# Three edits to the order of small operations in an attention and feed-forward kernel on one core

## The chip, the core and the metric

The kernel runs on one core of a Trainium2 chip. The metric is device time in microseconds (us) of one execution. Before the change it is 855.39 us, the median of three runs (854.91 to 855.95). The core has a matrix engine (PE; its weight loads are shown as PEld), a vector engine (DVE), a scalar engine (ACT), a general engine (POOL) and SyncE (SP), which issues nearly all DMAs. Each engine works through its own instructions in the order of the program and waits for the others by semaphores.

## The reference

Attention with softmaxes over q and over k, in 8 batches of 8 heads, 576 rows and 64 columns; its output, 4608 tokens of 512 columns, goes through a feed-forward layer with a squared ReLU.

```python
q_s = exp(q - max(q, -1)); q_s /= q_s.sum(-1) + 1e-9
k_s = exp(k - max(k, 2));  k_s /= k_s.sum(2) + 1e-9
kv  = einsum('bhsd,bhse->bhde', k_s, v)
x   = einsum('bhsd,bhde->bhse', q_s, kv).transpose(0, 2, 1, 3).reshape(4608, 512)
h   = maximum(x @ w_in, 0)          # w_in is 512 x 2048
out = (h * h) @ w_out               # w_out is 2048 x 512
```

## The kernel before

**Precision.** The feed-forward products keep single precision by splitting: an operand becomes a rounded part "hi" (a cast or copy on ACT) and a remainder "lo" = value minus hi (a subtraction on DVE, in a few places on POOL). A product is three matmuls: hi by hi, hi by lo, lo by hi.

**Tiles 0 to 4 (t = 0 to WT).** Five tiles of 512 tokens go straight through. Each has 16 chunks f of the hidden dimension. A chunk's order in the program (loop at L1631) is: `first`, 12 matmuls into a bank h, then ReLU and square on ACT into r; `sums_step`; `pairs_first`; the 12 matmuls of `second` for chunk f-2, in four output columns c; `split_g`, which makes gh (ACT) and gl (DVE) from r; `pairs_step`; in tile 4 also `ahead`.

**Attention for later batches runs inside tiles 1 to 4.** A round takes five chunks and serves two pairs of heads. In a tile, chunks 4, 9 and 14 are the last of a round, and hold `x_two` (L997), which stands between the columns c = 2 and c = 3 of `second`: PE multiplies q by kv, into a spare bank (the last 64 rows, tile h_x) and two other banks; ACT copies h_x to xt and the others to x. The next chunk's `first` writes into that spare bank (its matmuls are shown as h_x<-xh,w), so it waits for the copy xt. Chunks 3, 8 and 13 hold `blocks_norm` and `blocks_turn` (DVE: small bst operations, two products q<-q,bst, two transposes qT<-q) at their head, then `kv_of`: PE products kv from ek, DVE ks, ACT kv<-kv,ks; `x_two` needs these. Chunks 2, 7 and 12 hold the second `end_k` (DVE k shift, ACT ek).

**Sums of weights.** From tile 5 on pairs of tiles are done jointly by a seven-product (Strassen-Winograd) scheme, which needs sums of weight blocks. They are made in tiles 1 to 3, nine sets, three per tile (`SUMS_AT`, L1558), by `sums_step` (L1537): `full_sums` and `add_sums` on DVE, then at chunk 4, 9 or 14 `split_sums` (two ACT casts sums_h<-sums), one chunk later `rest_sums` (DVE), then `keep_sums` stores them (wo_sums<-sums_h). The buffers of all these have the tag "w" of a pool with two.

**Tile 4, `ahead` (L1579).** At the ends of chunks it makes the scheme's inputs of the first joint pair: blocks b11, b21, b12, b22 of x; t1 = b12-b11, t2 = b22-t1, t3 = t2-b11, t4 = b21-t2; each is split by `split_x_of` (two casts, two subtractions). t4's differences run on POOL.

**Joint pairs (k = 0, 1).** `first_products` (L1944) goes over eight pairs n of hidden chunks. A pair has seven products of six matmuls; p1, p6, p7 and p4 add up in bank A, p2, p5 and p3 in bank B, with an ACT copy u taken of A, and DVE sums c = B + u between them. Weights and sums for pair n+2 are loaded in pair n; a load own_a for the sums that are made on the spot comes with them, and DVE works on own_a in the pair after. `second_products` then does the second layer.

**Late outputs.** Of k = 0 five output blocks (out_N twice, c22[1], c21 twice) stay in memory and are turned during k = 1's `first_products`: `turned` (L1868) is a DVE transpose o<-c and four DMAs out_dram<-o of 128-byte runs. The transpose writes a tile of tag "gh", of which there are two; `pair_p4` takes its c from the same two. Two blocks go in n = 0, one each in n = 1, 2 and 3, right after p1. c22 is held in the ring "r" of two, where `pair_p2` also puts its c.

Of the kernel before, what the change touches and what calls it, by code (L numbers as in the profile page):

```python
# [336 lines left out]
def attention_ffn(  # L337
# [200 lines left out]
    made = {}  # L538
# [998 lines left out]
    def sums_step(t, f):  # L1537

        j, i = divmod(f, NF // 2)
        j += 2 * (t - 1)  # L1540
        if t >= 1 and j < NF // 2 and i == 3:
            begin_sums(j)
        for key, at in SUMS_AT.get(t, ()):
            if f == at[0]:
                full_sums(key)
            if f == at[1]:
                for n in range(3):
                    add_sums(key, n)
            if f == at[2]:
                add_sums(key, 3)  # L1550
                split_sums(key)
            if f == at[3]:
                rest_sums(key)
            if f == at[4]:
                keep_sums(key)

    THRICE = (2, 3, 4, 5, 6), (7, 8, 9, 10, 11), (12, 13, 14, 15, 15)
    SUMS_AT = {t: list(zip(KEYS[3 * t - 3:3 * t], THRICE)) for t in range(1, WT)}  # L1558
# [20 lines left out]
    def ahead(f, x):  # L1579

        k = range(2)
        if f == 4:
            made["b11"] = [x[:, i, :] for i in k]
            made["b21"] = [x[:, 2 + i, :] for i in k]
            made["b12"], made["b22"] = (
                [slabs[X_RAW + j].bitcast(F32)[:, i, :] for i in k] for j in range(2)
            )
            w_of[0] = weights(0)
            load_weights(0, w_of[0], "a11", "s1", "a12", "s2")
        elif f == 5:  # L1590
            for i in k:
                Y.dma_start(out=slabs[X_RAW + i].bitcast(F32), in_=x_raw[WT + 1, i])
        elif f == 6:
            split_x_of("b11")
        elif f == 8:
            one = cvt.tile([P, 2, M], F32, tag="w", name="t1_0")
            take("t1", V, [one[:, i, :] for i in k], made["b12"], made["b11"])
        elif f == 9:
            split_x_of("t1")
            take("t2", V, made["t1"], made["b22"], made["t1"])  # L1600
        elif f == 10:
            split_x_of("b21")
            take("t3", V, made["b11"], made["t2"], made["b11"])
        elif f == 12:
            split_x_of("t2")
        elif f == 14:
            take("t4", G, made["b21"], made["b21"], made["t2"])
            split_x_of("t3")
        elif f == 15:
            load_weights(0, w_of[0], "s3", "a22", "s4")  # L1610
            split_x_of("b22")
# [19 lines left out]
    for t in range(WT):  # L1631
        x_next, acc = x_tile(t + 1) if t < TB else None, begin_acc(t)
        parts = {}
        for f in range(NF):
            todo = turns[t, f] if t else None
            h = first(t, f, x)
            sums_step(t, f)
            if f < LA:
                parts[f] = split_g(t, f, *h)
            if t == 0:  # L1640
                for work in done:
                    convert(work, f + 1)
                plan.due = f + SOON
                step(1, f)
                plan.due = None
            if todo:
                pairs_first(*todo)
            if f >= LA:
                for c in range(C):
                    second_all(t, f - LA, parts[f - LA], acc, c)  # L1650
                    if c == 2 and todo and todo[1] > 2:
                        b, p = PAIRS_OF[todo[0]][1]
                        if todo[1] == 3:
                            kv_of(b, p - 1, p)
                        else:
                            x_two(b, p, x_next if b == TB else None)
                parts[f] = split_g(t, f, *h)
            if t == 0:
                plan.due = f + SOON
                step_after(1, f, x_next)  # L1660
                plan.due = None
            elif todo:
                pairs_step(*todo)
            if t >= TB and f == (5 if t == TB else 3):
                x_next = load_x(t + 1)
            if t == WT - 1:
                ahead(f, x_next)
        if t == 0:
            plan.run(SEEDS, fill)
        if t < WT - 1:  # L1670
            x = split_x(x_next, t + 1)
            end_tile(t, parts, acc, NF - 2, NF - 1)
            if t == 0:
                load_q(TB, 1)
                load_v(TB, 1)
                begin_k(TB, 0)
# [217 lines left out]
            out.append(u)  # L1894
        return out

    def added(bank_of, u, name):

        c = temp("r", name, bufs=None)
        V.tensor_tensor(out=c, in0=bank_of, in1=u, op=ALU.add)  # L1900
        return c

# [41 lines left out]
    def first_products(k):  # L1944

        old = None
        for n in range(PAIRS):
            if n == 0 and k == 0:
                split_x_of("t4")
                unit(3)  # L1950
            elif n == 0:
                begin_ring()
            z = pair_begin(n)
            pair_p1(z)
            if turned_late:
                turned_late.pop(0)()
            if n == PAIRS - 1:
                load_raw("b11", 1, raw_place("b11"))
            own_sums(n, z.w, 6)
            pair_p2(z)  # L1960
            if n == 0 and turned_late:
                turned_late.pop(0)()
            if n == PAIRS - 1 and k == 0:
                full_sums(late_key)
            if n == 0 and k == 0:
                unit(2)
                begin_ring()
            elif n == 0:
                split_x_of("t4")
                split_x_of("b22")  # L1970
            if old:
                pair_p4(old)
                load_weights(n + 1, w_of.get(n + 1), "a22")
                own_sums(n + 1, w_of.get(n + 1), 1)
                pair_p3(old)
                load_weights(n + 1, w_of.get(n + 1), "s4")
            own_sums(n + 1, w_of.get(n + 1), 2)
            if n == PAIRS - 1:
                load_raw("b11", 2, raw_place("b21"))
                split_step(0)  # L1980
            pair_p6(z)
            if old:
                pair_c12(old)
            own_sums(n + 1, w_of.get(n + 1), 3)
            if n == 0:
                unit(3)
            pair_p5(z)
            own_sums(n + 1, w_of.get(n + 1), 4)
            if n:
                own_sums(n + 2, None, 0)  # L1990
            if n + 2 < PAIRS:
                w_of[n + 2] = weights(n + 2)
                load_weights(n + 2, w_of[n + 2], "a11", "a12", "s2", "s1")
            elif n == PAIRS - 1:
                if k == 0:
                    for i in range(4):
                        add_sums(late_key, i)
                load_raw("b21", 0, raw_place("t2"))
                load_raw("b21", 1, raw_place("t2", 1))
                raw_x = att.tile([P, 4, M], F32, tag="x_next", name=f"raw_b12_{k}")  # L2000
                for j in range(2):
                    load_raw("b12", j, raw_x[:, 2 * j:2 * j + 2, :])
                split_step(1)
            pair_p7(z)
            load_weights(n + 2, w_of.get(n + 2), "s3")
            if n == PAIRS - 3:
                load_raw("b11", 0, *(temp("v", f"raw_b11_{k}_{i}", att, 2) for i in range(2)))
            if 0 < n < 5:
                load_s("s1", 2 * n - 2)
                if n < 4:  # L2010
                    load_s("s1", 2 * n - 1)
            elif n == PAIRS - 1:
                for j in range(2):
                    load_raw("b22", j, raw_place("t3", j))
            old = z
        return old

    def second_products(k, old):
# [26 lines left out]
        for s in range(1, 6 * J):  # L2045
# [21 lines left out]
            if s == 3 * J:  # L2067
                c11 = [added(out_B[m], u1[m], f"c11_{k}_{m}") for m in range(2)]
            elif s == 5 * J - 1:
                for m in range(2):  # L2070
                    turned(c11[m], two, m, "gh", None, (Y,))
            elif s == 5 * J:
                c22 = [added(out_N[m], u3[m], f"c22_{k}_{m}") for m in range(2)]
            elif s == 5 * J + 1:
                for m in range(2):
                    V.tensor_tensor(out=out_N[m], in0=out_N[m], in1=u2[m], op=ALU.add)
            elif s == 5 * J + 2:
                split_step(6 * J + 3)
                turned(c22[0], one, 2, "gh", None, (Y,))
# [84 lines left out]
```

## Time and profile before

| | |
|---|---|
| median of three runs | 855.39 us |
| the profiled execution: its own time, its span | 853.2 us, 851.4 us |
| PE, weight loads, DVE, ACT, POOL busy | 828.0, 664.0, 604.6, 494.3, 142.2 us |
| mean granted PE clock | 0.998 |
| DMA | 158.08 MB, 186 GB/s over the span |

The span runs from the first instruction to the last. A profile is one execution, slower or faster than the median by what single executions differ.

### The profile page before, as it was taken

The numbers are of one execution on the slowest core, as the hardware profiler recorded it, in microseconds if no ns is written. First come the engines' busy times: TensorE is split into PE (matmuls) and PEld (weight loads), VectorE is DVE, ScalarE is ACT, GpSimd is POOL, SyncE is SP. The second block draws the span as 40 slices with busy tenths as digits, with TensorE's granted clock in tenths as the row PEclk, the third lists the DMA queues.
The fourth block names the chain that finished last, engine by engine and source line by source line (L and its number), as shares of the span: only waits on it lengthen the run. The fifth ranks groups of instructions, "written<-read, shape, count | busy, mean of one in ns | idle before, by whom it ended". The sixth has DMA issues, their size and how long they took to land.

```text
span 851.4 us, 12950 instructions
## 1 busy us (share of the span) xinstructions
PE 828.0 (97%) x4411; PEld 664.0 (78%) x4411; DVE 604.6 (71%) x1098; ACT 494.3 (58%) x890; POOL 142.2 (17%) x153
## 2 busy tenths in 40 slices
PE   8999999899999999999999999999999999899997
PEld 7677777688887787787787787888888877688886
DVE  6888965676675685675665585477698977676984
ACT  5988844545555547555555466466754546575442
POOL 4888980001000000000000001000210000000000
PEclk9999999999999999999999999999999999999999
DMA  9993124426536537355536542899866689989455
GB/s 291 378 343 90 31 42 117 105 77 170 148 107 165 134 126 220 82 173 134 154 136 145 192 126 70 271 291 307 298 255 196 199 248 272 287 294 358 127 175 95
DMA packets 230146, 158.08 MB, mean 186 GB/s; under 512 B 147392, under 2 KB 200128, under 8 KB 230080
## 3 DMA queue, kind: packets, MB, share of 16 engines
q1 hardware_dynamic: 224160, 155.55, 60.3%
q10 hardware_dynamic: 5920, 1.71, 0.9%
q8 instruction: 35, 0.57, 0.3%
q14 instruction: 31, 0.25, 0.1%
HBM read 106.95 MB, written 49.81 MB: 184 GB/s over the span
## 4 chain that ended last, share of the span: by engine, by line
PE 59%; DVE 15%; DMA 10%; ACT 6%; SPq 5%; issue 4%; POOL 0%; DVEq 0%; ACTq 0%; POOLq 0%
PE acc L100 14%; PE out L1839 14%; PE h L1302 13%; PE h L100 11%; SPq L100 5%; PE h_x L100 4%; DVE bst L100 4%; DVE q L100 3%; DMA k<-in_k_dram 3%; DVE w L100 2%; DMA own_a<-w_sums 1%; ACT r L100 1%; PE x L100 1%; PE kv L100 1%; DVE qT L100 1%
## 5 line engine op out<-in xcount | busy, mean ns | idle before, releaser
L100 PE MATMUL acc<-w,gh 128*128 128x512 f32 x632 | 198.5, 395 | 0.0
L100 PE MATMUL h<-xh,w 128*128 128x512 f32 x544 | 179.6, 393 | 0.8 <-ACT xh L100 0.8
L1839 PE MATMUL out<-w,w 128*128 128x512 f32 x636 | 148.9, 389 | 0.0
L100 PEld LDWEIGHTS acc<-w,gh 128*128 128x128 f32 x632 | 116.1, 188 | 29.6 <-issue 5.9
L1839 PEld LDWEIGHTS out<-w,w 128*128 128x128 f32 x636 | 119.3, 188 | 25.1 <-DVE w L100 0.2
L100 DVE TENSOR_TENSOR gl<-r,gh 128x512 fp32r<-128x512 f32 x64 | 44.2, 690 | 112.0 <-ACT gh L100 112.0
L100 PE MATMUL acc<-w,gl 128*128 128x512 f32 x316 | 123.1, 389 | 0.0
L100 PEld LDWEIGHTS h<-xh,w 128*128 128x128 f32 x544 | 102.1, 188 | 23.5 <-ACT xh L100 1.3
L100 PE MATMUL h<-xl,w 128*128 128x512 f32 x272 | 106.3, 391 | 0.1
L100 POOL PARTITION_ALL_REDUCE kmx<-km x24 | 22.7, 946 | 361.8 <-DVE km L100 361.8
L1302 PE MATMUL h<-w,w 128*128 128x512 f32 x288 | 69.6, 390 | 1.0 <-DMA w<-w_sums 1.0
L100 PEld LDWEIGHTS acc<-w,gl 128*128 128x128 f32 x316 | 59.3, 188 | 12.5
L1302 PEld LDWEIGHTS h<-w,w 128*128 128x128 f32 x288 | 53.9, 188 | 13.0 <-DMA w<-w_sums 1.5
L100 PEld LDWEIGHTS h<-xl,w 128*128 128x128 f32 x272 | 51.1, 188 | 11.9 <-DVE xl L100 1.5
L100 ACT ACTIVATE c<-c 128x512 f32<-128x512 f32 x76 | 48.1, 633 | 19.8 <-DVE c L100 18.2
L100 ACT ACTIVATE kv<-kv,ks 64x64 f32<-64x64 f32 x64 | 19.8, 309 | 58.7 <-DVE ks L100 56.7
L100 ACT CAST gh<-r 128x512 fp32r<-128x512 f32 x64 | 39.7, 621 | 17.0 <-PE acc L100 15.4
L1302 PE MATMUL h<-w,ring 128*128 128x512 f32 x192 | 46.7, 391 | 2.8 <-DMA ring<-w_sums 1.7
L100 ACT ACTIVATE q<-q 128x576 f32<-128x576 f32 (+1 forms) x32 | 21.5, 672 | 46.7 <-DVE q L100 39.3
L100 ACT CAST w<-w 128x1024 fp32r<-128x1024 f32 (+1 forms) x38 | 37.9, 1003 | 15.2 <-PE out L1839 8.7
L100 DVE TENSOR_TENSOR c<-h,u 128x512 f32<-128x512 f32 x48 | 33.0, 687 | 18.1 <-ACT u L100 17.0
L100 ACT ACTIVATE r<-h 128x512 f32<-128x512 f32 x68 | 40.1, 590 | 9.2 <-PE h L100 8.6
(229 smaller groups left out, 1387.9 us busy)
## 6 DMA issues: line engine op xcount, KB each, us to landing
w<-wo_sums SPq DMA_DIRECT2D x64, 256.0 KB, 3.4
g_b<-c SPq DMA_DIRECT2D x60, 256.0 KB, 4.2
w<-g_b SPq DMA_DIRECT2D x18, 512.0 KB, 7.1
raw<-in_moe_w_in_dram SPq DMA_DIRECT2D x16, 512.0 KB, 8.1
raw<-in_moe_w_out_dram SPq DMA_DIRECT2D x16, 512.0 KB, 8.6
w<-w_sums SPq DMA_DIRECT2D x32, 256.0 KB, 5.0
w_sums<-w SPq DMA_DIRECT2D x30, 256.0 KB, 3.2
v<-in_v_dram SPq DMA_DIRECT2D x56, 128.0 KB, 3.1
```

The lines of the kernel that those rows point to most:

```text
L100: getattr(self.eng, op)(*map(real, args), **{k: real(a) for k, a in kwargs.items()})
L1302: nc.tensor.matmul(out=out.real(), lhsT=a[:, k * P:(k + 1) * P].real(), rhs=m[k].real(), start=(begin and k == 0 and i == 0), stop=(k == 1 ...
L1839: nc.tensor.matmul(out=banks[name][m].real(), lhsT=a[:, m * P:(m + 1) * P].real(), rhs=b[:, i, :].real(), start=fresh and j == i == k == 0 ...
```

## The change

Three edits. (1) `split_sums` is taken out of `sums_step` and called from a new `sums_after` at the end of the same chunk, behind `second`, `x_two`, `split_g` and `pairs_step`. (2) In `ahead`, b11's split and t1's differences move to the end of chunk 7 (from 6 and 8), t3's differences to chunk 12 ahead of t2's split (from 10), and t4's differences go from POOL to DVE, behind t3's split. (3) The late outputs skip pair n = 1: c22[1] goes in n = 2 and c21 in n = 3 and 4; c22[1] is held in the tile "qt".

```diff
             if f == at[2]:
                 add_sums(key, 3)
-                split_sums(key)
...
+    def sums_after(t, f):
+
+        for key, at in SUMS_AT.get(t, ()):
+            if f == at[2]:
+                split_sums(key)
...
-        elif f == 6:
+        elif f == 7:
             split_x_of("b11")
-        elif f == 8:
             one = cvt.tile([P, 2, M], F32, tag="w", name="t1_0")
             take("t1", V, [one[:, i, :] for i in k], made["b12"], made["b11"])
...
         elif f == 10:
             split_x_of("b21")
+        elif f == 12:
             take("t3", V, made["b11"], made["t2"], made["b11"])
-        elif f == 12:
             split_x_of("t2")
         elif f == 14:
-            take("t4", G, made["b21"], made["b21"], made["t2"])
             split_x_of("t3")
+            take("t4", V, made["b21"], made["b21"], made["t2"])
...
                 pairs_step(*todo)
+            sums_after(t, f)
...
-    def added(bank_of, u, name):
+    def added(bank_of, u, name, place=("r", ffn, None)):
 
-        c = temp("r", name, bufs=None)
+        tag, pool_of, bufs = place
+        c = temp(tag, name, pool_of, bufs)
...
-            if turned_late:
+            if n != 1 and turned_late:
                 turned_late.pop(0)()
...
-                c22 = [added(out_N[m], u3[m], f"c22_{k}_{m}") for m in range(2)]
+                c22 = [
+                    added(out_N[0], u3[0], f"c22_{k}_0"),
+                    added(out_N[1], u3[1], f"c22_{k}_1", ("qt", att, 1)),
+                ]
```

## Rows read from the trace of the kernel before

**Rows 1.** The page: busy us of each engine (share of the span), instructions.
```profile
PE 828.0 (97%) x4411; PEld 664.0 (78%) x4411; DVE 604.6 (71%) x1098; ACT 494.3 (58%) x890; POOL 142.2 (17%) x153
```

**Rows 2.** PE's waits over the span: waiting line, releaser, us in total, times, longest.
```profile
PE h_x L100 <- ACT xt L100: 4.3, 5, 1.0
```

**Rows 3.** Timeline, tile 1, chunk 4: start, us, engine, operation, count, [idle before, releaser].
```profile
161.99 1.12 ACT L100 CAST sums_h_i<-sums_i 128x512 fp32r<-128x512 f32 x2
...
163.01 0.26 ACT L100 COPY xt<-h_x 128x128 f32<-128x128 f32 x1
...
163.32 0.50 PE L100 MATMUL h_x<-xh,w 128*128 128x512 f32 x1 [1.03 <-ACT xt L100]
...
166.39 0.60 ACT L100 ACTIVATE r<-h_x 128x512 f32<-128x512 f32 x1 [0.80 <-PE h_x L100]
```

**Rows 4.** Timeline, tile 2, chunks 7 and 8.
```profile
280.11 1.29 DVE L100 TENSOR_TENSOR full_o<-w 128x512 f32<-128x512 f32 x2 [2.05 <-DMA wo_sums<-sums_h_o]
...
282.65 0.63 ACT L100 ACTIVATE ek<-qn 128x512 f32<-128x512 f32 x1 [4.02 <-DVE qn L100]
...
283.47 0.34 PE L100 MATMUL kv<-v,ek 128*64 128x65 f32 x6
```

**Rows 5.** Timeline, tile 4, chunks 6 to 9.
```profile
477.72 1.28 DVE L100 TENSOR_TENSOR w<-x,w 128x512 fp32r<-128x512 f32 x2
...
480.23 0.63 ACT L100 ACTIVATE ek<-qn 128x512 f32<-128x512 f32 x1 [3.90 <-DVE qn L100]
...
480.91 0.69 PE L100 MATMUL kv<-v,ek 128*64 128x65 f32 x16 [0.59 <-ACT ek L100]
...
482.25 0.47 DVE L100 TENSOR_TENSOR bst<-bst 128x36 f32<-128x36 f32 x2 [1.85 <-DMA bst<-bst]
...
484.19 1.43 DVE L100 TENSOR_TENSOR q<-q,bst 128x576 f32<-128x576 f32 x2
...
487.66 0.60 PE L100 MATMUL h_x<-qT,kv 64*64 64x64 f32 x3 [0.28 <-ACT kv L100]
```

**Rows 6.** Timeline, tile 4, chunks 12 to 15.
```profile
512.90 1.29 DVE L100 TENSOR_TENSOR w<-t,w 128x512 fp32r<-128x512 f32 x2 [1.35 <-ACT w L100]
...
516.04 2.52 DVE L100 TENSOR_TENSOR q<-q,bst 128x576 f32<-128x576 f32 x2
...
516.49 3.22 POOL L100 TENSOR_TENSOR x<-x,t 128x512 f32<-128x512 f32 x2 [6.92 <-issue]
...
520.60 0.60 PE L100 MATMUL h_x<-qT,kv 64*64 64x64 f32 x3 [1.50 <-ACT kv L100]
...
530.22 0.69 DVE L100 TENSOR_TENSOR gl<-r,gh 128x512 fp32r<-128x512 f32 x1 [2.35 <-ACT gh L100]
```

**Rows 7.** Timeline, joint pair k = 1, n = 1.
```profile
700.66 0.71 DVE L100 STREAM_TRANSPOSE o<-c 128x512 f32<-128x512 f32 x1 [5.16 <-DMA out_dram<-o]
...
702.09 1.67 PE L1302 MATMUL h<-w,ring 128*128 128x512 f32 x6 [1.14 <-DVE c L100]
...
702.73 0.60 ACT L100 ACTIVATE c<-h 128x512 f32<-128x512 f32 x1 [5.42 <-DMA out_dram<-o]
...
704.51 1.66 PE L1302 MATMUL h<-w,ring_s 128*128 128x512 f32 x6 [0.75 <-ACT u L100]
704.62 0.43 DVE L100 TENSOR_TENSOR own_k<-w 128x256 f32<-128x256 f32 x1 [0.59 <-DMA w<-w_sums]
```

**Rows 8.** Timeline of PE and DVE, k = 1, n = 4 to 6.
```profile
726.27 3.04 PE L1302 MATMUL h<-w,w 128*128 128x512 f32 x12 [1.04 <-DMA w<-w_sums]
...
737.43 0.69 DVE L100 TENSOR_TENSOR own_a<-own_a 128x512 f32<-128x512 f32 x1 [4.05 <-DMA own_a<-w_sums]
...
738.06 3.02 PE L1302 MATMUL h<-w,ring 128*128 128x512 f32 x12 [1.67 <-DMA ring<-w_sums]
...
746.40 0.69 DVE L100 TENSOR_TENSOR own_a<-own_a 128x512 f32<-128x512 f32 x1 [1.22 <-DMA own_a<-w_sums]
...
748.00 2.88 PE L1302 MATMUL h<-w,w 128*128 128x512 f32 x12
```

## The prediction, made before the changed kernel was run

> **What bounds the kernel now.** The page comes first: PE is busy in 828.0 us of a span of 851.4, 97%, and the next engine, DVE, in 71% [rows 1]. So PE sets the time, and only what shortens PE's gaps can shorten the run. Second come PE's waits: the largest is "h_x for ACT xt", 4.3 us in five waits of at most 1.0 [rows 2]. Third, the timeline around each gap, to see which instruction stood last before PE was let go [rows 3 to 8]. Taken together, the gaps that the three edits can touch are: 4.3 us for xt; 0.59, 0.28 and 1.50 us in tile 4, 2.4 in all [rows 5, 6]; 1.14 and 0.75 in pair n = 1, 1.04 and 1.67 at the heads of n = 4 and n = 5, 4.6 in all [rows 7, 8]. That makes 11.3 us; the question is how much of it is really lost for good.
>
> **Part 1, the rounding of the sums.** In chunk 4 of tile 1 ACT does the two casts of the sums from 161.99, and only then the copy xt, at 163.01; PE has waited 1.03 for that copy and begins at 163.32 [rows 3]. With the casts behind, xt starts 163.01 - 161.99 = 1.02 sooner, and the wait all but disappears. The reader is to see that nothing else stands in between: the casts start as soon as the square before them is done, and xt as soon as the casts are. Of the five waits four have this size (4 x 1.03 = 4.1 of 4.3); I leave the fifth, 0.2, where it is, since there xt is held back by the kv work ahead of it on ACT too. There are nine such casts in tiles 1 to 3; in the other four chunks PE comes to xt later than the casts end, and nothing is won. Gross: 4 x 1.02 = 4.1.
>
> What the moved casts cost: they now stand behind gh of the same chunk and ahead of the next ReLU. ACT has an idle stretch of 0.80 there [rows 3]; in the four chunks PE brings that ReLU forward by 1.02 and the casts' end stays, so the ReLU comes about 0.3 late. It frees a bank that PE asks for two chunks later: the 12 matmuls that end with this ReLU's release take 3.0 us (163.32 to about 166.37 [rows 3]), a chunk has 24, so there are several us of cover; without it the price is 0.3 in each. Behind them DVE's `rest_sums` is queued, which DVE reaches only after gl and a k maximum: no wait.
>
> What is late next: in tile 2 DVE stands 2.05 us for a transfer, the store of the chunk-4 sums, whose buffer the next set takes over; DVE goes on at 280.11, and so ek is only done at 282.65 + 0.63 = 283.28, 0.19 before PE uses it at 283.47 [rows 4]. The store is issued by SP behind a row of loads that began before `x_two`, so it doesn't come sooner when PE does. PE will arrive 1.02 earlier, at 282.45, and wait until 283.3: 0.85 goes back. That place lies between the second and the third of the four gains, and is the only kv product in tiles 1 to 3 that I found this tight. Net of part 1: 4.1 - 0.85 = **3.2**. Ends: all 4.3, with nothing late next; or below nothing, 9 x (1.02 - 0.80) = 2.0 lost, if every set pushes its ReLU past ACT's idle stretch and PE feels it.
>
> **Part 2, the differences in tile 4.** b11's two subtractions (477.72, 1.28 us) leave chunk 6, where gl, the k shift and ek stand behind them; ek, at 480.23, comes about 1.2 sooner and PE's wait of 0.59 goes [rows 5]. But they come back in chunk 7 with t1's two differences behind them, and in front of chunk 8's bst work. From ek at 479.0 (480.23 - 1.2): ek 0.63, the k tail about 0.2, the first of two casts 0.6 (half of a pair like that in [rows 3]), so the subtractions start about 480.4; these and t1's pair, 1.28 each but overlapping a little, last until about 482.8. bst now starts at 482.25 behind an idle of 1.85 that a transfer ends [rows 5]. So it starts 0.55 later, and everything hangs on it: the products, the transposes, ks, kv and PE's h_x at 487.66, which already waits 0.28. PE's h_x therefore comes at 488.2, 0.55 later than now, although PE itself is there 0.59 earlier.
>
> t3's pair goes to chunk 12, into an idle of 1.35 in which DVE waits for ACT's casts [rows 6]; two differences of this shape take 1.28 to 1.29, so it just fits, and frees at most 0.1 in chunk 10. t4's pair goes to DVE behind t3's split, where DVE is idle for 2.35 ahead of gl at 530.22 [rows 6]: nothing, or 1.29 if that idle were gone.
>
> The other side of t4's move: two q products in chunk 13 take 2.52 while POOL's two differences run from 516.49 for 3.22 us [rows 6]; the same two take 1.43 in chunk 8 [rows 5]. The excess, 2.52 - 1.43 = 1.09, lies on the path to h_x at 520.60, which waits 1.50. One long pair could be chance, or POOL's doing. The Trainium skill, page SBUF — State Buffer, section Who interferes with whom, has a rule for it: a DVE instruction with two SBUF inputs and a GpSimd instruction that reads SBUF exclude each other, and whichever is second stands still until the first is done. By that rule the whole 1.09 goes with POOL's work, as in my sum; were it chance, the sum would be 1.1 us smaller. This trace agrees as far as one pair can.
>
> h_x in chunk 14: 0.55 later, 0.1 and 1.09 sooner. Net of part 2: 1.09 + 0.1 - 0.55 = **0.6**. Ends: 2.4, all three waits; or 0.55 lost, if the 1.09 stays.
>
> **Part 3, the late outputs.** In n = 1 DVE stands 5.16 us at the transpose for a "gh" tile that an output DMA still reads, and ACT 5.42 at p4's c for the other one [rows 7]. Without this block DVE runs on, and PE's wait of 1.14 for c goes. p4's c now takes the tile that frees at 700.6 instead of 702.7, so ACT is 2 us sooner and PE's 0.75 goes too. The gain of 1.9 is cut at once: n = 2's first weights land at 704.6 [rows 7], and nothing brings them forward. PE now begins n = 2 about 1.5 after 704.51 (six matmuls), at 706.0; it could be there about 2 sooner, but begins at 704.6, 1.4 sooner.
>
> Then it is the transfers' turn. PE's heads of n = 4 and 5 are both ended by weight loads, 738.06 - 726.27 = 11.79 apart; without a late block in the pair before, own_a comes 746.40 - 737.43 = 8.97 after the last [rows 8]. A block so costs the chain of loads 2.8 per pair. The change takes one block out ahead of n = 3 and puts one in ahead of n = 6: own_a for n = 3 comes 2.8 sooner, then three intervals of 11.79 follow instead of two and one of 8.97, and n = 6's loads land when they do now, at 746.4 and the weights about 0.7 later. PE began n = 6 at 748.00 without a wait; at best it begins at 747.1. Net of part 3: **0.9**. The transposes themselves, 0.71 each, keep their place on DVE one pair later, between idle stretches of some us; c22[1]'s new tile has no user there. Ends: 4.6, all four waits; or 2.8 lost, if the third block comes on top of the loads that n = 4 and 5 issue.
>
> **Sum.** 3.2 + 0.6 + 0.9 = 4.7. The profiled execution took 853.2, 1.8 more than its span; 853.2 - 4.7 = 848.5. It lies 2.2 below the median of 855.39, which is what will be compared: 855.39 - 4.7 = **850.7**.
>
> **Rivals.** A change within 0.2%, 1.7 us, can't be told from none here.
>
> *Nothing is given back.* Parts 1 and 3 keep 4.3 and 1.9, part 2 0.59 + 1.09 + 0.1: 8.0, so 847.4. For it: PE is nearly always the last. Against: the row of 280.11, a chain tied to a transfer. Chance 0.18.
>
> *Most is given back.* PE's gains in one chunk are eaten in the next, wherever k, sums or weights hang on transfers as in [rows 4]: part 1 keeps 4 x (1.02 - 0.85) = 0.7, parts 2 and 3 nothing. 854.7. For it: three of the rows 4 to 8 show DVE or PE held by a DMA. Against: only the one kv product of [rows 4] has its ek so shortly before its use. Chance 0.20, two fifths of it still faster.
>
> *The change doesn't do what it says:* xt waits for kv work and not for the casts, and part 1 is nothing. 855.39 - 1.5 = 853.9. Against: the casts and xt are back to back in [rows 3]. Chance 0.05.
>
> *Slower.* The casts, now between gh and the next ReLU, hold that ReLU in all nine chunks, and PE with it: 9 x 1.02 = 9.2 lost against 4.1 won, 5.1 less 1.5 from the other parts: 859.0. It decides from the point where the ReLU behind the casts is the last thing that PE's next free bank waits for. ACT's idle there is only 0.80; against it stands the cover of two chunks. Chance 0.07.
>
> **How the numbers follow.** Forecast 0.50, with a range of its own of 849.2 to 852.4 (part 1 between 2 and 4, part 3 between 0 and 2). Adding the case of nothing given back reaches down to 847.2, and most of the give-back case up to 854.4. Faster: 0.50 + 0.18 + 0.08 = 0.76. Same: 0.12 + 0.05 = 0.17. Slower: 0.07.
>
> **What would show it.** In the changed kernel's profile: PE's waits for xt fall from 4.3 to under 0.6; a new wait "kv for ek" of about 0.85 in tile 2's chunk 8. In tile 4: no wait for ek, one of over 1.3 at h_x in chunk 9, the q products of chunk 13 at about 1.43, and a wait of about 0.5 in chunk 14. In k = 1: no DVE wait for out_dram in n = 1, own_a intervals of about 11.8 three times, PE waiting for weights at n = 5 and 6. I am wrong if xt still waits, if DVE's waits for sums_h appear, or if the last pair starts later against n = 0 than now.

## The result, and the profile after

The changed kernel takes 847.71 us (median of 4 runs, 846.02 to 849.88) against 855.22 (4 runs, 854.91 to 855.95): ratio 0.9912 [0.9889, 0.9936], 7.5 us faster where 4.7 were forecast. A second comparison gave 850.18 (9 runs) against 855.37 (20 runs), 5.2 us by the medians; its ratio of 0.9943 [0.9922, 0.9965] makes it 4.9. The first profiled execution took 847.65, its span 845.8, against 853.2 and 851.4: 5.6. The forecast of 850.7 lies 0.5 above the second median and 3.0 above the first; which parts brought the gain is another matter.

The page after, busy time of each engine, answers to [rows 1]. PE does the same work in a shorter span; only POOL has lost something, t4's two differences:

```profile
PE 828.0 (98%) x4411; PEld 663.4 (78%) x4411; DVE 604.9 (72%) x1100; ACT 494.9 (59%) x890; POOL 139.0 (16%) x151
```

PE's waits after, answering to [rows 2] (waiting line, releaser, us in total, times, longest):

```profile
PE kv L100 <- ACT ek L100: 2.7, 2, 1.7
PE h_x L100 <- ACT kv L100: 2.0, 1, 2.0
PE h L1302 <- DMA w<-w_sums: 2.0, 3, 1.0
...
PE kmT L100 <- DVE sm L100: 1.0, 1, 1.0
...
PE h L1302 <- DMA ring<-w_sums: 0.4, 1, 0.4
PE h L1302 <- ACT u L100: 0.3, 1, 0.3
```

The row for xt is gone from the list. What stands there now names the places where part of the gain went back: ek, kv, and the weights of the joint pairs; of the 2.7 for ek, 1.7 in tile 1 was there before.

*Tile 1, chunk 4* (timeline: start, us, engine, operation, count), answering to [rows 3]. xt follows the square with no cast between, and PE begins without a wait, 2.08 earlier by the clock of the trace, of which 1.05 came from ahead of this place. The casts now stand behind gh, and the next ReLU follows them without idle time:

```profile
160.94 0.25 ACT L100 COPY xt<-h_x 128x128 f32<-128x128 f32 x1
...
161.24 0.50 PE L100 MATMUL h_x<-xh,w 128*128 128x512 f32 x1
...
163.41 1.14 ACT L100 CAST sums_h_i<-sums_i 128x512 fp32r<-128x512 f32 x2
...
164.46 0.59 ACT L100 ACTIVATE r<-h_x 128x512 f32<-128x512 f32 x1
```

*Tile 2, chunks 7 and 8*, answering to [rows 4]. full_o waits 3.33 for the same store, ek comes when that lets it, and PE now waits 0.98 where it had not waited:

```profile
278.09 1.29 DVE L100 TENSOR_TENSOR full_o<-w 128x512 f32<-128x512 f32 x2 [3.33 <-DMA wo_sums<-sums_h_o]
...
280.62 0.63 ACT L100 ACTIVATE ek<-qn 128x512 f32<-128x512 f32 x1 [5.30 <-DVE qn L100]
...
281.30 0.69 PE L100 MATMUL kv<-v,ek 128*64 128x65 f32 x16 [0.98 <-ACT ek L100]
```

*Tile 4, chunks 6 to 9*, answering to [rows 5]. In the kernel before, DVE's k maximum waits 2.95 for the load of k:

```profile
475.72 1.09 DVE L100 TENSOR_REDUCE km<-qn 128x128 f32<-128x512 f32 x1 [2.95 <-DMA qn<-in_k_dram]
```

Now it waits 3.71, so ek is not 1.2 sooner but 0.65, beyond the 4.23 by which PE was ahead here; behind it the casts, b11's and t1's subtractions follow each other, bst starts straight behind them with no idle time left, and PE's h_x waits 2.02:

```profile
472.04 1.09 DVE L100 TENSOR_REDUCE km<-qn 128x128 f32<-128x512 f32 x1 [3.71 <-DMA qn<-in_k_dram]
...
475.35 0.63 ACT L100 ACTIVATE ek<-qn 128x512 f32<-128x512 f32 x1 [4.47 <-DVE qn L100]
...
476.08 1.12 ACT L100 CAST w<-x 128x512 fp32r<-128x512 f32 x2
...
476.72 1.29 DVE L100 TENSOR_TENSOR w<-x,w 128x512 fp32r<-128x512 f32 x2 [1.20 <-ACT w L100]
477.93 1.29 DVE L100 TENSOR_TENSOR t<-w,x 128x512 f32<-128x512 f32 x2
479.13 0.46 DVE L100 TENSOR_TENSOR bst<-bst 128x36 f32<-128x36 f32 x2
...
484.53 1.27 PE L100 MATMUL h_x<-qT,kv 64*64 64x64 f32 x7 [2.02 <-ACT kv L100]
```

From 1.48 behind that wait's end the granted clock is at half, 1.2 GHz, for 3.41 us. Three stretches of equal length, before, in and after it (busy time, PEclk, DMA share): PE is full in the second and third, yet the work of the second took 1.14 us longer than the same matmuls did in the trace of before:

```profile
482.50:485.90 3.40, 1.34 (x16) 1.00 0.39 64
486.01:489.42 3.41, 3.41 (x18) 0.50 0.77 132
489.50:492.90 3.40, 3.40 (x17) 1.00 0.87 257
```

*Chunks 13 to 15*, answering to [rows 6]. The q products take 1.43 instead of 2.52, h_x starts without a listed wait, and t4's differences on DVE leave 0.85 of idle time ahead of gl:

```profile
513.41 1.43 DVE L100 TENSOR_TENSOR q<-q,bst 128x576 f32<-128x576 f32 x2
...
517.19 0.97 PE L100 MATMUL h_x<-qT,kv 64*64 64x64 f32 x7
...
524.09 1.29 DVE L100 TENSOR_TENSOR x<-x,t 128x512 f32<-128x512 f32 x2
526.23 0.69 DVE L100 TENSOR_TENSOR gl<-r,gh 128x512 fp32r<-128x512 f32 x1 [0.85 <-ACT gh L100]
```

*Joint pairs of k = 1*, answering to [rows 7, 8]. The waits of 1.14 and 0.75 in n = 1 shrink to 0.29 in all; PE then waits at the heads of n = 2, 4, 5 and 6, each for weights:

```profile
699.12 1.66 PE L1302 MATMUL h<-w,ring_s 128*128 128x512 f32 x6 [0.29 <-ACT u L100]
701.75 1.42 PE L1302 MATMUL h<-w,w 128*128 128x512 f32 x5 [0.96 <-DMA w<-w_sums]
...
721.78 1.43 PE L1302 MATMUL h<-w,w 128*128 128x512 f32 x5 [0.65 <-DMA w<-w_sums]
...
732.27 0.96 PE L1302 MATMUL h<-w,ring 128*128 128x512 f32 x3 [0.44 <-DMA ring<-w_sums]
...
742.73 0.96 PE L1302 MATMUL h<-w,w 128*128 128x512 f32 x3 [0.35 <-DMA w<-w_sums]
```

To see where the time went, each PE matmul of one trace is set beside the same one of the other, and the difference of their starts followed along the run. From before to after it moves by -1.0 up to 81 us (no edit is there), -3.2 in tiles 1 to 3, +0.5 in tile 4 (-0.6 without the half-clock stretch), and -1.25 over the joint pairs; the last 0.6 of the span's 5.6 lies in the products and stores at the end.

### The profile page after: what moved, and what is told of

Its sections match the earlier page's. It is cut to its first block, busy times and chain, and to the rows that moved or that the text cites. A ratio compares the mean times of both kernels' runs of the same rounds, so it can differ in the third digit from the quotient of the medians.

```text
span 845.8 us, 12951 instructions
## 1 busy us (share of the span) xinstructions
PE 828.0 (98%) x4411; PEld 663.4 (78%) x4411; DVE 604.9 (72%) x1100; ACT 494.9 (59%) x890; POOL 139.0 (16%) x151
## 4 chain that ended last, share of the span: by engine, by line
PE 79%; DMA 8%; DVE 5%; SPq 3%; ACT 2%; issue 1%; DVEq 0%; ACTq 0%
PE acc L100 21%; PE out L1844 18%; PE h L100 17%; PE h L1302 14%; PE h_x L100 5%; SPq L100 3%; DMA w<-w_sums 3%; PE x L100 2%; PE kv L100 2%; DMA raw<-in_moe_w_in_dram 2%; DMA k<-in_k_dram 2%; DVE bst L100 1%; DVE q L100 1%; DMA own_a<-w_sums 1%; DMA w<-x_raw 0%
```

## The experiments

*Three single parts.* Each is the kernel before with one part of the diff alone: the moved casts, the lines of `ahead`, the late outputs with c22[1]'s tile. The first:

```diff
-                split_sums(key)
...
+            sums_after(t, f)
```

> Only the rounding casts of the weights' sums are moved behind the chunk; tile 4 and the late outputs stay as before. Theory A (the gaps add up as the two traces show): PE's waits for xt fall from 4.3 to under 0.6 us; in tile 2, chunk 8, a new wait of kv for ek of about 1.0; from the start of tile 1 to the start of tile 4 PE is 3.2 us ahead of before, and tile 4 and the joint pairs keep their waits (0.59, 0.28, 1.50; 1.14, 0.75, 1.04, 1.67 within a few tenths). Time 3 us below before. Rival B (this edit alone is the whole result, the other two nothing): 7 us below before. Rival C (the gain is eaten in later chunks): under 1.5 us.

Measured: 851.61 (9 runs) against 855.73 (27), ratio 0.9940 [0.9919, 0.9961]; the four xt waits give 1.23, 1.17, 0.90 and 0.98, the kv product in tile 2 takes 0.76 back, and PE is 3.5 us ahead by the end of tile 3: theory A by the trace. The time doesn't decide: 4.1 us by the medians, 5.1 by the ratio, lies between A's 3 and rival B's 7, and the interval, 3.3 to 6.9 us, leaves out both by little. The later waits didn't stay within a few tenths, as A had it: ek waits 0.09, n = 1 1.87, n = 4 1.90, n = 5 0.41.

The trace also shows what the casts cost in their new place. Here, in tile 1, chunk 4, ACT still idles 0.15 behind them, for PE, so the ReLU behind them isn't late (timeline of ACT, casts alone):

```profile
165.20 1.14 ACT L100 CAST sums_h_i<-sums_i 128x512 fp32r<-128x512 f32 x2
166.50 0.60 ACT L100 ACTIVATE r<-h_x 128x512 f32<-128x512 f32 x1 [0.15 <-PE h_x L100]
```

In three other chunks of this trace, and in four of the nine in the first trace of the changed kernel, the one shown above among them, the ReLU has no idle time ahead of it. It then starts 0.55 to 0.58 behind the start of the bank's last matmul instead of 0.43, so it is 0.12 to 0.15 late. No listed wait of PE is for it.

The second:

```diff
-        elif f == 6:
+        elif f == 7:
             split_x_of("b11")
-        elif f == 8:
...
-            take("t4", G, made["b21"], made["b21"], made["t2"])
             split_x_of("t3")
+            take("t4", V, made["b21"], made["b21"], made["t2"])
```

> Only the edits of tile 4. Theory A: the wait of kv for ek in chunk 8 (0.59) goes or falls under 0.2, but h_x in chunk 9 waits about 2 us instead of 0.28, because b11's subtractions and t1's differences stand ahead of chunk 8's bst work on DVE; where that wait is 2 us long the granted PE clock falls to half for some 3 us behind it and another 1.1 us is lost; h_x in chunk 14 waits about 0.2 to 0.5 instead of 1.50. Over tile 4 PE is between 0.6 us ahead (no fall of the clock) and 0.5 us behind. Time within 1 us of before. Rival B (tile 4 brings most of the result's 7.5 us): 3 us or more below before.

Measured: 855.34 (12 runs), ratio 0.9992 [0.9970, 1.0014]: PE gains 0.71 at the kv product, loses 0.87 at h_x of chunk 9 and about 1.2 in a half-clock stretch behind it, and gains 1.7 at chunk 14. Theory A, but for a size: h_x of chunk 9 waits 1.19, not about 2. Alone, part 2 is worth nothing that can be measured.

The third:

```diff
-            if turned_late:
+            if n != 1 and turned_late:
                 turned_late.pop(0)()
...
+                    added(out_N[1], u3[1], f"c22_{k}_1", ("qt", att, 1)),
```

> Only the late outputs' turn in pairs n = 2 to 4. Theory A: in k = 1 PE's waits of 1.14 and 0.75 in n = 1 go (at most 0.3 left), n = 2 gets a wait for its weights of about 1.0, n = 4, 5 and 6 wait about 0.65, 0.45 and 0.35; own_a arrives in intervals of over 10.5 us up to n = 6. At the start of n = 6 PE is 1.0 to 1.5 us ahead of before. Time 1 us below before. Rival B (the two waits of n = 1 are won for good): 1.9 us or more ahead at n = 6, 2 us below before. Rival C (a block costs its pair the same wherever it stands): nothing.

Measured: 853.58 (12 runs), ratio 0.9974 [0.9951, 0.9996]; about 1.3 us earlier by the end of n = 6. Theory A, but n = 4 has no wait where 0.65 was expected. (This trace also gains 1.1 in chunk 14 of tile 4, which no edit of this part touches; see the second trace of before.) By the ratios the three reductions, 0.60, 0.08 and 0.26%, add up to 0.94%, beside 0.88 and 0.57% for all three together: with about 0.2% of uncertainty in each, the parts don't hinder each other by more than these can tell.

*t4's differences back on POOL*, all else as changed.

```diff
-            take("t4", V, made["b21"], made["b21"], made["t2"])
+            take("t4", G, made["b21"], made["b21"], made["t2"])
```

> The changed kernel with t4's two differences on POOL again, all else as changed. Theory A (POOL's two differences stop one of DVE's q products in chunk 13): the two q products take about 2.5 us again instead of 1.43, h_x in chunk 14 starts about 1.1 us later relative to h_x in chunk 9, and the time is 1 us above the changed kernel's, 6.5 below before. Rival B (the long q product was chance): q products at 1.43 with POOL busy beside them, and the time of the changed kernel. If POOL's work, now behind t3's split in chunk 14, no longer meets the q products of chunk 13, neither shows, and the price of POOL is then only where it stood.

Measured: 849.29 (7 runs), ratio 0.9929 [0.9903, 0.9955]. POOL starts 0.52 behind the start of the q products and these take 2.52 again; h_x waits 1.40: theory A by the trace, while the time, between the two medians of the changed kernel, can't tell 1 us. Timeline, chunks 13 and 14:

```profile
513.32 2.52 DVE L100 TENSOR_TENSOR q<-q,bst 128x576 f32<-128x576 f32 x2
...
513.84 3.14 POOL L100 TENSOR_TENSOR x<-x,t 128x512 f32<-128x512 f32 x2 [6.98 <-issue]
...
517.88 0.66 PE L100 MATMUL h_x<-qT,kv 64*64 64x64 f32 x4 [1.40 <-ACT kv L100]
```

*Three further moves*, each on the changed kernel, each aimed at one of the waits that it brought: b11's split from chunk 7 to the end of chunk 5; the load of the next x in tile 2 from chunk 5 to 6, so behind the store of the sums; the output DMAs of pair 2's late block behind that pair's weight loads. Then all three.

```diff
 e5:      elif f == 5: ...
+            split_x_of("b11")
         elif f == 7:
-            split_x_of("b11")
 e6:
-            if t >= TB and f == (5 if t == TB else 3):
+            if t >= TB and f == (6 if t == TB else 3):
 e7:
-            if n == 0 and turned_late:
-                turned_late.pop(0)()
+            held_out = turned_late.pop(0)() if n == 0 and turned_late else None
...
+            if held_out is not None:
+                turned_out(held_out, JOINT[0][0], 1, (Y,))
             pair_p7(z)
```

> The changed kernel with one line moved: b11's two subtractions of tile 4 stand at the end of chunk 5 instead of at the head of chunk 7, where DVE has an idle stretch of nearly 3 us ahead of the k maximum. Theory A: the h_x wait of chunk 9 (2.03 in the changed kernel) is the price of b11's pair in chunk 7, which holds bst; moved, that wait falls to 0.6 to 1.2, ek still comes in time (no kv wait above 0.3 in chunk 7), and the half-clock stretch behind that wait goes with it: PE is 0.8 to 3 us earlier from chunk 9 of tile 4 on, some 845 to 847 us in all. Theory B: t1's pair alone, or the transfer that bst waits for, holds bst: the h_x wait stays at 1.8 or more and the time at 847 to 849. Theory C: the idle stretch in chunk 5 is not free, the k maximum and ek slip by 1.2 and the kv wait of 0.6 is back: no gain.

Measured: 848.46 (6 runs), ratio 0.9924 [0.9898, 0.9951]. In the trace theory A, and more: the h_x wait falls from 2.02 to 0.31, there is no half-clock stretch, and PE is 2.7 earlier over tile 4; bst now waits 1.70 for its transfer, which is the next limit. About 1.2 of the 2.7 goes back in the joint pairs, and this execution had started 1.7 later, so the gain can't be told in its time. Timeline, chunks 7 to 9:

```profile
475.87 1.28 DVE L100 TENSOR_TENSOR t<-w,x 128x512 f32<-128x512 f32 x2
478.85 0.46 DVE L100 TENSOR_TENSOR bst<-bst 128x36 f32<-128x36 f32 x2 [1.70 <-DMA bst<-bst]
...
484.26 0.93 PE L100 MATMUL h_x<-qT,kv 64*64 64x64 f32 x5 [0.31 <-ACT kv L100]
```

> The changed kernel with the load of the next x in tile 2 issued in chunk 6 instead of chunk 5, behind the store of the sums. Theory A: DVE's wait of 2 us for that store in tile 2, chunk 7, comes from the store standing behind that row of loads on SP's queue; with the store first, ek is done at least 1 us sooner and the kv wait of 0.98 in tile 2, chunk 8, goes: 0.8 to 1.1 us from there on, with x's copies of the next tile still in time. Theory B: the store is late for another reason (the sums themselves, the other queues): the kv wait stays at 0.7 or more. Theory C: the later load makes the next tile's copies late: a new wait at the head of tile 3 of more than 0.5, no gain.

Measured: 848.38 (6 runs), ratio 0.9922 [0.9898, 0.9947]. In tile 2 theory A: full_o waits no longer, PE's wait of 0.98 is gone, and no wait appears at tile 3. PE is 2.4 earlier by 355 us, of which about 1.4 comes behind the wait itself and isn't explained, and 3.5 by the end of tile 4, but gives 2.5 back in the joint pairs, most of it in n = 1, 4 and 5, where it waits for u and for weights. Timeline, tile 2, chunks 7 and 8:

```profile
275.13 1.28 DVE L100 TENSOR_TENSOR full_o<-w 128x512 f32<-128x512 f32 x2
...
280.60 0.64 PE L100 MATMUL kv<-v,ek 128*64 128x65 f32 x16
```

> The changed kernel with the four output DMAs of the late block of pair 2 issued behind that pair's weight loads instead of ahead of them. Theory A: the weight wait of 0.96 at the start of pair 2 comes from these output DMAs standing ahead on the queue: it falls below 0.2, and own_a for pair 3 is held instead by the output behind it, so PE gains 0.5 to 1 at pair 2 and gives 0 to 1 of it back by pair 6. Theory B: the loads are late because of the transfers still in flight from the pair before, not the order of issue: the wait stays at 0.8 or more and nothing moves. Theory C: the output now collides with the loads of pair 3: the wait at pair 4 or 5 grows by more than 1.

Measured: 848.20 (6 runs), ratio 0.9915 [0.9887, 0.9943]. The wait at n = 2 is gone, but in this execution PE waited 2.02 for u in n = 1 (ACT stood 5.25 at p4's c for an output transfer, 3.51 in the changed kernel) and came later to all that follows, so alone it settles nothing.

> The changed kernel with all three moves at once: b11 in chunk 5, the load of x in chunk 6 of tile 2, the late output's DMAs behind the weights. Theory A: the gains stand at separate places and add: 1.1 + 0.8 (more if the half-clock stretch goes too) + 0.5, so 2 to 4 us below the changed kernel, 844 to 846 us, and a ratio against the kernel before of 0.987 to 0.989. Theory B: they are given back by the next limit, a weight load or a kv product: 847 to 848, ratio 0.990 to 0.992.

Measured: 844.00 (6 runs, 840.60 to 846.28) against 855.77 (11), ratio 0.9869 [0.9839, 0.9900]. Against the changed kernel PE gains 2.2 by the end of tile 2, 2.8 in tile 4, and 2.4 over the joint pairs, where the wait at n = 2 is gone although PE arrives 5 us earlier. So theory A for all three: in the same comparison the single moves stand at 848.2 to 848.5, some 4 us above. The trace reads as if the gains add once the heads of the joint pairs are eased too, but no run has two of the moves, so which one keeps the others' gains isn't shown; and this trace is of the fastest of the six executions. What is left of the waits above:

```profile
PE kv L100 <- ACT ek L100: 1.7, 1, 1.7
...
PE h_x L100 <- ACT kv L100: 0.7, 2, 0.4
PE h L1302 <- DMA ring<-w_sums: 0.7, 1, 0.7
PE h L1302 <- DMA w<-w_sums: 0.5, 1, 0.5
```

*Both kernels again, unchanged*, for a second trace of each.

> The kernel before, unchanged, for a second trace of it. Theory A: the 2 us by which the changed kernel won more than its trace shows come from executions that differ (arrival of the first loads of k, stretches at half clock), not from the edits: the five waits for xt (4.3 us), the ek and h_x waits of tile 4 and the waits of n = 1, 4 and 5 come back within 0.4 each, while the start (to 80 us) or a half-clock stretch moves the span by 1 to 4 us, to 852 to 855. Theory B: the first trace of before missed something that the edits remove: gaps between 150 and 750 us differ from it by more than 1.5 us in sum, without a half-clock stretch. The ratio is 1.000 within 0.003.

Measured: 854.73 (12 runs, 851.49 to 859.77), ratio 0.9993 [0.9969, 1.0016]; the profiled execution took 859.77, its span 858.0, 6.6 longer than the first. Each theory has a part of it. 3.9 us are there by 61 us, as theory A has it: PE waits 3.44 for DVE at the k maximum of tile 0, 3.1 more than in the first trace, and a half-clock stretch that begins 0.14 before the wait ends costs another 1.4 (PE had been 0.5 ahead until there). DVE stands 3.33 us for the load of q ahead of it; over the 13 traces PE's wait here runs from none to 3.4, whatever the kernel. But from there to 750 us the two traces of one kernel move apart by another 3.1 us with no half-clock stretch, which is theory B's sign: n = 3 has a new wait of 0.71, n = 4 waits 1.73 instead of 1.04, and smaller ones grow, while the waits for xt come back. Timeline of the second trace of before, DVE and PE at 50 to 58 us:

```profile
50.02 0.69 DVE L100 TENSOR_REDUCE mx<-q 128x8 f32<-128x512 f32 x1 [3.33 <-DMA q<-in_q_dram]
...
57.62 0.45 PE L100 MATMUL kmT<-ident,km 128*128 128x128 f32 x1 [3.44 <-DVE sm L100]
```

And one row overturns a step of the forecast. In this execution POOL runs the same two differences, but starts 0.94 behind the start of the q products instead of 0.45; these take 1.43, and h_x waits 0.39 instead of 1.50:

```profile
521.08 1.43 DVE L100 TENSOR_TENSOR q<-q,bst 128x576 f32<-128x576 f32 x2
...
522.02 2.87 POOL L100 TENSOR_TENSOR x<-x,t 128x512 f32<-128x512 f32 x2 [7.42 <-issue]
...
524.55 1.27 PE L100 MATMUL h_x<-qT,kv 64*64 64x64 f32 x7 [0.39 <-ACT kv L100]
```

The late outputs alone, also with POOL at this work, show the same at 1.10:

```profile
516.76 1.43 DVE L100 TENSOR_TENSOR q<-q,bst 128x576 f32<-128x576 f32 x2
...
517.86 2.72 POOL L100 TENSOR_TENSOR x<-x,t 128x512 f32<-128x512 f32 x2 [7.58 <-issue]
```

> The changed kernel, unchanged, for a second trace of it and for a ratio on the same chip as the next run. Theory A: median 847 to 849, ratio 0.990 to 0.993; from 81 us to the last pair PE stands 3.8 to 5.0 us earlier against the new trace of before, plus what half-clock stretches make of it (about 1.6 us each); h_x of chunk 9 in tile 4 waits 1.7 to 2.2 again, with or without a half-clock stretch behind it. Theory B: the changes of part 2 and 3 were chance of one execution: the sum from 81 us differs from 4.5 by more than 1.5 with no half-clock stretch in either.

Measured: 850.18 (9 runs), ratio 0.9943 [0.9922, 0.9965]. Neither theory holds as written. The median is above the band, and between the two new traces the sum from 81 us is about 7 us, although this trace has a half-clock stretch at 157 us that costs it 1.6. The four xt waits give 4.5, the kv product takes 1.5 back, tile 4 gives nothing (-1.33, then +1.26; chunk 14 had only 0.39 of wait to lose), and the joint pairs give 3.2, since before's waits there were larger in its second trace. h_x of chunk 9 waits 1.28, not 2.02.

*All three moves, and late blocks in pairs 2, 4 and 5.*

```diff
-            if n != 1 and turned_late:
+            if n not in (1, 3) and turned_late:
```

> The kernel with all three moves, and the late output blocks in pairs 2, 4 and 5 instead of 2, 3 and 4. Theory A: a late block costs the chain of weight loads about 2.8 us, and a pair without one gives it back: own_a comes about 9.0 after the last one for the pair behind a free pair 3, the head wait at n = 5 (0.83 in the kernel with all three moves) falls under 0.3, the one at n = 6 stays at 0.5 to 1.0 as it now has a block ahead: 0.3 to 0.8 gained, 843 to 844.5. Theory B: the head waits come from the ring loads and not from the blocks: no head wait moves by more than 0.2 and the time is the same. Theory C: two blocks on end ahead of n = 6 push its loads more than 1 us late: 0.5 to 1.5 slower.

Measured: 845.01 (6 runs), ratio 0.9883 [0.9863, 0.9904]: no better than the 844.00 with blocks in 2, 3 and 4, as far as two comparisons can tell. Behind the free pair own_a comes after 8.88 us, and the wait at n = 5 (0.67 in the trace of all three moves) goes, as theory A has it; but the one at n = 6, which A had stay, goes too. The two blocks that follow then make intervals of 10.6 and 10.7, and n = 7 waits 1.40: what theory C named, one pair later. The wait moved two pairs on. Timeline of DVE and PE, n = 4 to 7:

```profile
719.01 0.69 DVE L100 TENSOR_TENSOR own_a<-own_a 128x512 f32<-128x512 f32 x1 [3.69 <-DMA own_a<-w_sums]
...
727.89 0.69 DVE L100 TENSOR_TENSOR own_a<-own_a 128x512 f32<-128x512 f32 x1 [1.17 <-DMA own_a<-w_sums]
...
749.20 0.69 DVE L100 TENSOR_TENSOR own_a<-own_a 128x512 f32<-128x512 f32 x1 [2.89 <-DMA own_a<-w_sums]
...
750.70 3.04 PE L1302 MATMUL h<-w,ring 128*128 128x512 f32 x12 [1.40 <-DMA ring<-w_sums]
```

## Why the prediction was right, and where it was not

*The time.* 850.7 was forecast, 847.71 and 850.18 measured. The two differ by 2.5, more than parts 2 and 3 together were forecast to bring, which shows how far a median of four runs carries here. The second, with more runs, gives 4.9 to 5.2 against the 4.7 of the sum, but that is luck in part: from 81 us to the last pair the first two traces differ by 3.95 (3.2, -0.5 and 1.25 for the parts), the second two by about 7.

*Part 1: right in mechanism and size.* "xt starts 1.02 sooner" holds at four places in each of the three traces that can show it. The fifth wait, 0.2, which the sum left in place, went as well. Gross 3.9 to 4.5 was measured where 4.1 was forecast, given back 0.76 to 1.5 at the one kv product that was named where 0.85 was forecast; net 3.2 in the first pair of traces, as in the sum. The cause given for that kv product, the store behind a row of loads, is shown: with the load of x behind the store, the wait goes. The rival "the casts hold the next ReLU, and PE with it" falls: where they hold it, it is 0.12 to 0.15 late, where 0.3 had been allowed, and PE doesn't wait. "xt waits for kv work" falls with the missing row.

*Part 2: wrong by 1.1 us, which the total hides.* The step "ek comes about 1.2 sooner" failed: the k maximum ahead of it waits for the load of k, and this load let it go only 3.68 sooner where PE was 4.23 ahead; ek gained 0.65. So bst came 1.1 later against PE's work instead of 0.55 (479.13 beside 482.25 - 4.23 = 478.02, with 4.23 the lead that PE had by then), h_x of chunk 9 waited 2.02, and the half-clock stretch behind that wait, which no step had, cost 1.14 more. Against that, chunk 14 came 1.73 sooner against 1.74 in the sum: 0.6 gained was forecast, 0.5 lost measured in the first pair of traces, 0.1 gained in the second, nothing to be measured alone. The run with b11 moved ahead shows that its place is the cause: there the wait is 0.31. But 2.02 is among the longest: in the six executions that have b11 in chunk 7, h_x waits 1.19, 1.28, 1.35, 1.75, 2.02 and 2.04, around the 1.42 that the sum implies (0.28 + 0.59 + 0.55), and a half-clock stretch follows in four of them. That stretch is the term that the sum lacked.

What the sum took from the 1.09 was right in cause, and "by chance" was right as well. In the five traces with t4's differences on POOL, a start 0.39, 0.45 and 0.52 us behind the q products goes with 2.52, a start 0.94 and 1.10 behind with 1.43. The Trainium skill, page SBUF — State Buffer, section Who interferes with whom, says that a DVE instruction with two SBUF inputs, as the q products are, and a GpSimd (POOL) instruction that reads SBUF exclude each other; these rows agree: it is the second product that is long, 1.84 instead of 0.75, and only where POOL starts ahead of it (the second starts 0.68 behind the first). So the 1.09 that the sum took as certain is there in three of five executions.

*Part 3: right in mechanism, two terms mis-sized.* The 1.9 of n = 1 was won (1.88), and n = 2's loads cut it as forecast, but deeper: PE waits 0.96 there and keeps 0.75, not 1.4. The "three intervals of 11.79" didn't come: they were 12.62, 10.58 and 10.04, so n = 6's loads came earlier than the sum had them, and PE waits 0.65, 0.44 and 0.35 at n = 4, 5 and 6, beside 1.04 and 1.67 before. Forecast 0.9, measured 1.25, 1.3 alone, 3.2 in the second pair, where the kernel before had waited longer: the two errors pull opposite ways.

*What of the rivals on what is given back?* "Most is given back" named the right mechanism, chains tied to transfers, and the further moves show it at work: the later load of x gained 3.5 and gave 2.5 back. In tile 4 of the first trace it even held, with 2.4 gained and 2.9 lost. For the change as a whole it fell, since part 1 kept 3.2. "Nothing is given back" forecast 847.4, and the first median, 847.71, is nearer to that than to 850.7; by the time alone it would have won. The traces refute it: 1.16 goes back at tile 2's kv product, all of tile 4's gain, 1.1 at n = 2.

*Open.* Why the first comparison gave 7.5 and the second about 5 isn't settled. The wait at 54 us, the half-clock stretches and POOL's start each move one execution by 1 to 4 us, and four runs may draw them unevenly; no run tells this apart from a difference between chips. What makes the load of q late in some executions wasn't tried.

## What to carry to other kernels

An in-order engine that is half idle can still be the limit, by what it does in the microsecond before the busy engine asks: find the instruction that stood last, and move work that nobody waits for behind it. Before adding up such gains, mark on each chain the first instruction that a transfer releases: PE's lead is safe only up to there. The later load of x, alone and with the other two moves, shows microseconds lost and kept by what stood at the next transfers. One profile is one execution: a wait that lies at the mercy of a start 0.5 us earlier or later, as POOL's here, should enter a sum with a chance and not as a fixed price.

## What the runs showed of the hardware

*The clock after a single wait.* Between 50 and 800 us the 13 traces have 12 stretches at half clock (1.2 GHz), each 3.41 us long, each beginning within 2.1 us of a PE wait or in one. None of 49 waits of 0.5 to 1.15 us has such a stretch behind it, 6 of 41 between 1.15 and 2.0 have, and 6 of 7 above 2.0. The same wait of 1.74 in tile 1 stands in all 13 traces and is followed by one in three. A stretch cost 1.1 to 1.6 us on top of a wait of 1.19 to 3.44. So in this kernel a PE wait near 2 us was often dearer than its length, although PE is busy in 97% of the span.

*The spread of one kernel.* 27 runs of the kernel before on one chip went from 851.89 to 859.94 us. The two traces of it differ by 6.6 us in span: 3.9 of it by 61 us, from one wait behind a late load and the half-clock stretch that begins in it, and most of the rest from small waits between 350 and 750 us.
